# Strassen's seven products for a feed-forward output matmul, with weight combinations streamed from device memory

## The chip, the cores and the metric

One core of one Trainium2 chip runs the kernel. Its engines work side by side: TensorE (PE; its weight loads are listed apart as PEld), VectorE (DVE), ScalarE (ACT), GpSimd (POOL) and SyncE (SP), whose queue issues all DMA transfers here. The metric is the device time of one execution in microseconds (us). A time is a median of several runs. The profile comes from one further execution, and sums are made against that one's own time.

## The reference

Linear attention over 8 batches x 8 heads x 576 tokens x 64 dimensions, then a feed-forward layer with the Mish activation over the 4608 tokens that it gives. All arrays are float32.

```python
def phi(x):
    proj = np.einsum('bhsd,df->bhsf', x, w_phi)               # 128 features
    proj = proj - np.max(np.abs(proj), axis=-1, keepdims=True)
    return np.concatenate([np.exp(proj), np.exp(-proj)], axis=-1)
q_p, k_p = (phi(q), phi(k))
kv = np.einsum('bhsf,bhsd->bhfd', k_p, v)
z = np.sum(k_p, axis=2)
num = np.einsum('bhsf,bhfd->bhsd', q_p, kv)
den = np.einsum('bhsf,bhf->bhs', q_p, z)[..., None] + 1e-06
x = num / den                                                 # as 4608 tokens x 512
h = x @ w_in                                                  # 512 x 2048
sp = np.where(h > 20.0, h, np.log1p(np.exp(np.minimum(h, 20.0))))
out = (h * np.tanh(sp)) @ w_out                               # 2048 x 512
```

## The kernel before

**Tiling.** The 4608 tokens are 18 chunks of 256. For each chunk `c` the layer makes 16 feature tiles of 128 (`in c f`): `h` = `w_in` times `x`, 12 matmuls of 256 columns. Two tiles share a PSUM bank, and for each such pair ACT applies Mish (`mish`, giving `u`). `out c f` multiplies the tile's features with 128 rows of `w_out` into two banks `o`, one for each 128 tokens of the chunk, 512 columns wide, which add up over all 16 tiles. `evict` copies them out and `store` sends them off.

**Three products for one.** Both matmuls of the layer work on numbers split in a high part, rounded to a shorter float, and a low part, the rest: `gh` is a rounding cast of `u` on ACT, `gl` is `u - gh` on DVE, and high x high, high x low and low x high are added. The weights are split once, early in the run, on DVE and ACT, from the 64-bit words in which they come. Each piece of `w_out` lies in SBUF as a tile `wout` of high and low part side by side, 128 x 2 x 512, for all the run.

**Attention** runs beside the layer, in units: 36 units of keys (`k0` to `k35`) and 18 x 2 units of queries (`q c g`). A unit is loaded (`raw`), projected on PE into two banks (`pp`), centred on DVE (maxima `m`, then `e`) and put through two exponentials on ACT. For keys, `sum` adds up products with `v` in a bank `kvps`, one bank for each of the 32 pairs of heads and batches, which DVE copies to `kv`. For queries, `e` is first transposed: DVE transposes blocks, and a round trip through device memory (`there`) sorts them. Then `num` makes two banks of products with `kv`, DVE divides, and another round trip, a cast on ACT and a subtraction on DVE give `xTh` and `xTl`, which `h` reads. In the steady part one unit of queries and one of keys go by for every four pairs of feature tiles.

**Banks.** PSUM has eight: four `att` (attention's), two `h` (the layer's first product, and some projections) and two `o`.

**Order.** Nothing is scheduled while it runs. Each step is a task with an engine, a key (a place on a common scale, one unit for each feature tile), a duration, tasks it depends on, and ring places that it takes and gives back. `Plan.order` plays the tasks through once, and the program is written down in the order found. Each engine follows its own list strictly, and so does SP's queue of transfers: whoever waits holds up all that stands behind it.

## Time and profile before

| | |
|---|---|
| median of 3 runs | 1082.2 us (1082.09 to 1083.13) |
| the profiled execution | 1082.3 us, of which 1080.5 us from its first to its last instruction |
| mean granted TensorE clock | 0.996 |
| PE busy | 1061.9 us, 98% |
| DVE busy | 539.9 us, 50% |
| ACT busy | 666.3 us, 62% |
| data moved by DMA | 120.11 MB, mean 111 GB/s |

A matmul's busy time in the groups of instructions (282 ns for 256 columns) overlaps with the next one's, since they are pipelined. What one costs in a row of them is read from the chain in order of time, where a piece of twelve has its length. In rows, `h<-xTh,win` stands for an output tile and the tiles read, `128x256` for partitions x elements, `x12` for a count, and what stands behind `<-` in brackets for whom the engine waited.

### The profile page before, as it was taken

Reading aid. Unit: us, or ns where it says so; the run is one execution under the profiler, and the core shown is the slowest. Engines: PE = TensorE matmul, PEld = TensorE weight load, DVE = VectorE, ACT = ScalarE, POOL = GpSimd, SP = SyncE. Lnnn points to the kernel's source line nnn. Section 1 sums busy time; section 2 is a strip of 40 time slices with the busy share of each in tenths; the row PEclk is TensorE's granted clock in tenths of the full one; section 3 lists DMA queues with packets and bytes.
Section 4 is the critical chain, followed back from the end, with each engine's and each line's share of the span. In section 5 each row is a group of like instructions: output and inputs, shape, how many; then the busy total and the mean of one; then the engine's idle time right before and its main releaser. Section 6 shows DMA issues by size and latency. Waiting matters only on the chain.

```text
span 1080.5 us, 26883 instructions
## 1 busy us (share of the span) xinstructions
PE 1061.9 (98%) x11272; PEld 963.2 (89%) x11272; DVE 539.9 (50%) x1184; ACT 666.3 (62%) x1013; POOL 0.7 (0%) x6
## 2 busy tenths in 40 slices
PE   7799999999999999999999999999999999999998
PEld 7789988899999999999999999999999999889897
DVE  7899997444444544443444444444444443434211
ACT  6598998656666666666666666666666664444412
POOL 0000000000000000000000000000000000000000
PEclk9899999999999999999999999999999999999999
DMA  9568743333232223232323223232323222222100
GB/s 354 203 233 288 272 137 122 100 92 111 92 110 76 92 87 102 78 102 86 101 91 98 93 91 99 91 111 79 104 78 107 62 83 83 92 77 92 35 20 20
DMA packets 94009, 120.11 MB, mean 111 GB/s; under 512 B 10432, under 2 KB 56640, under 8 KB 93888
## 3 DMA queue, kind: packets, MB, share of 16 engines
q1 hardware_dynamic: 93888, 118.38, 33.1%
q8 instruction: 89, 1.46, 0.6%
q14 instruction: 32, 0.26, 0.1%
HBM read 85.31 MB, written 33.03 MB: 110 GB/s over the span
## 4 chain that ended last, share of the span: by engine, by line
PE 89%; ACT 6%; DVE 3%; issue 1%; DMA 1%; SPq 0%; ACTq 0%; DVEq 0%
PE h L445 34%; PE o L480 34%; PE kvps L289 7%; PE num L289 6%; PE pp_q L266 3%; PE pp_k L266 3%; ACT L451 1%; ACT u L451 1%; ACT wout L234 1%; ACT L182 1%; PE dt L350 0%; ACT gh L454 0%; DMA raw_k<-kT 0%; ACT w_out L182 0%; ACT e_q L360 0%
## 5 line engine op out<-in xcount | busy, mean ns | idle before, releaser
L445 PE MATMUL h<-xTh,win 128*128 128x256 f32 x2304 | 460.3, 282 | 1.3 <-ACT u L451 1.3
L445 PEld LDWEIGHTS h<-xTh,win 128*128 128x128 f32 x2304 | 374.0, 188 | 17.0 <-ACT u L451 1.5
L480 PE MATMUL o<-wout,gh 128*128 128x512 f32 x1152 | 362.3, 395 | 0.6 <-ACT wout L234 0.6
L445 PE MATMUL h<-xTl,win 128*128 128x256 f32 x1152 | 324.9, 282 | 0.3 <-DVE xTl L429 0.3
L462 DVE TENSOR_TENSOR gl<-u,gh 128x256 fp32r<-128x256 f32 x288 | 111.4, 422 | 389.3 <-ACT gh L454 386.9
L480 PE MATMUL o<-wout,gl 128*128 128x512 f32 x576 | 226.8, 394 | 0.0
L445 PEld LDWEIGHTS h<-xTl,win 128*128 128x128 f32 x1152 | 216.4, 188 | 10.7 <-DVE xTl L429 0.5
L480 PEld LDWEIGHTS o<-wout,gh 128*128 128x128 f32 x1152 | 197.3, 188 | 29.3 <-ACT wout L234 1.3
L324 ACT ACT_TABLE_LOAD x50 | 64.2, 1283 | 202.4 <-DVE e_k L281 201.9
L451 ACT ACTIVATE u<-h 128x512 f32<-128x512 f32 x144 | 86.2, 599 | 140.5 <-PE h L445 124.1
L480 PEld LDWEIGHTS o<-wout,gl 128*128 128x128 f32 x576 | 108.0, 187 | 26.6
L451 ACT ACT_TABLE_LOAD x94 | 120.6, 1283 | 1.7
L454 ACT CAST gh<-u 128x256 fp32r<-128x256 f32 x288 | 105.4, 404 | 7.9
L289 PEld LDWEIGHTS kvps<-v,e_k 128*64 128x64 f32 x2560 | 77.9, 137 | 9.6 <-issue 6.5
L289 PE MATMUL kvps<-v,e_k 128*64 128x66 f32 x2560 | 82.8, 223 | 1.6 <-issue 1.6
L289 PE MATMUL num<-kv,e_q 128*64 128x66 f32 x2304 | 76.5, 224 | 0.5 <-ACT e_q L360 0.5
L289 PEld LDWEIGHTS num<-kv,e_q 128*64 128x64 f32 x2304 | 72.2, 139 | 4.3 <-ACT e_q L360 1.5
L324 ACT ACTIVATE e_k<-e_k 128x512 f32<-128x512 f32 x72 | 45.3, 629 | 8.3 <-DVE e_k L281 7.8
L273 DVE TENSOR_REDUCE m_k<-pp_k 128x4 f32<-128x512 f32 x72 | 45.9, 677 | 7.5 <-PE pp_k L266 7.4
L266 PE MATMUL pp_k<-w_phi,raw_k 64*128 64x128 f32 x560 | 44.5, 292 | 4.5 <-DMA raw_k<-kT 4.5
L325 ACT ACTIVATE e_k<-e_k 128x512 f32<-128x512 f32 x72 | 45.5, 632 | 2.3
L266 PEld LDWEIGHTS pp_k<-w_phi,raw_k 64*128 64x128 f32 x560 | 40.8, 201 | 6.0 <-issue 4.8
(59 smaller groups left out, 725.5 us busy)
## 6 DMA issues: line engine op xcount, KB each, us to landing
there_e<-e_q SPq DMA_DIRECT2D x60, 256.0 KB, 2.1
e_q<-there_e SPq DMA_DIRECT2D x240, 64.0 KB, 2.0
v<-va SPq DMA_DIRECT2D x32, 330.0 KB, 3.4
raw_q<-qT SPq DMA_DIRECT2D x36, 256.0 KB, 3.0
out<-osb SPq DMA_DIRECT2D x36, 256.0 KB, 2.1
raw_k<-kT SPq DMA_DIRECT2D x35, 256.0 KB, 3.0
words_in<-w_in SPq DMA_DIRECT2D x16, 512.0 KB, 6.0
words_out<-w_out SPq DMA_DIRECT2D x16, 512.0 KB, 4.9
```

Of the source, the lines that this page charges most:

```text
L182: nc.scalar.activation(w.bitcast(F32), high.bitcast(F32), AF.Abs)
L234: nc.scalar.copy(both((kind, i, j))[0], to_add.pop((kind, i, j)).bitcast(F32))
L266: nc.tensor.matmul(ps[j][:, n], raw[rows, n * P:(n + 1) * P], w_phi2[rows], start=True, stop=True)
L273: nc.vector.tensor_reduce(ms[j], ps[j], axis=AX.X, op=ALU.max, apply_absolute_value=True)
L289: nc.tensor.matmul(ps[rows], lhsT[h], rhs[h], start=start, stop=stop, skip_group_check=True)
L324: nc.scalar.activation(e[:, 1, :], e[:, 0, :], AF.Exp)
L325: nc.scalar.activation(e[:, 0, :], e[:, 0, :], AF.Exp, scale=-1.0)
L445: nc.tensor.matmul(ps, w[:, wcol], x[:, cc % 2, :], start=(n == 0), stop=(n == 11))
L451: nc.scalar.activation(u, h_live.pop((c, fp)).rearrange("p f s -> p (f s)"), AF.Mish)
L454: nc.scalar.copy(gh, u[:, f * CH:(f + 1) * CH])
L462: nc.vector.tensor_sub(gl, u[:, f * CH:(f + 1) * CH], gh.bitcast(F32))
L480: nc.tensor.matmul(ps, g[:, cols], w, start=(i == first and k == 0), stop=(i == end and k == 2))
```

## The change

From chunk 5 on (`FAST`), each pair of feature tiles is seen as a 2 x 2 block product: two blocks of 128 tokens, two of 128 features, two of 256 output columns. Strassen's scheme forms it with seven block products in place of eight. Each is again three matmuls (high and low parts), now 256 columns wide, and adds into one of four banks over the chunk's eight pairs: `x` and `z` take the two `o` banks, `y` and `w` take two of the four `att` banks, which attention gives up from chunk 5 on.

- *Per pair.* ACT: `mish`, one cast `gh` (256 columns: two of the four blocks), one cast `sh` (640 columns: the five sums). DVE: three instructions for the five sums `s`, one `gl`, and `sl` = `s - sh` (640 columns).
- *Per chunk.* ACT copies the `x` bank; DVE combines the four banks with eight additions of 256 columns into `osb0` and `osb1`, which are stored.
- *Weights.* Five combinations of the blocks of `w_out` are needed for each pair. Once, around chunks 1 to 5, DVE and ACT form them and 48 transfers write them to device memory (`terms`). Later each is loaded again for each chunk and pair, 520 loads of 256 KiB, into halves of the `wout` tiles: the scheme uses only one half of each piece, and the other becomes one of 16 homes, filled in turn.
- *Order.* Rings are resized (`part` holds eight places of 640 columns, in place of five of 512; `kv` and `half` lose two places and one). A query or key unit's centring is split in four tasks from step 12 on; a unit's `sum` is one task for each pair of heads, and from pair 11 on the two parts of a pair's sum are made in banks of their own, the second being added to `kv` on DVE. The planner may hold PE up to 0.4 on its scale for the next `sum`, `num` or `project`.

The places on each engine where this shows follow; in the listings `x2` or `x4` merges equal neighbours, and numbers in names are chunk, pair or unit, with a running number last.

TensorE (PE) before, chunk 9, at the end of a group of queries: the last `num` products, the projections of queries `q10_1` and of keys `k26`, and the next feature tile.

```order
L289 MATMUL num1_10_0_7625<-kv_17_5869,e1_q10_0_7325 64x66 x4
L266 MATMUL pp0_q10_1_7647<-w_phi2_81,raw_q10_1_7462 128x128
L266 MATMUL pp1_q10_1_7648<-w_phi2_81,raw_q10_1_7462 128x128
...
L266 MATMUL pp0_k26_7663<-w_phi2_81,raw_k26_7460 128x128
L266 MATMUL pp1_k26_7664<-w_phi2_81,raw_k26_7460 128x128
...
L445 MATMUL h_9_4_7683<-xTh_9_0_7057,win_0_1_1071 128x256
```

TensorE (PE) after, the same place.

```order
L322 MATMUL kvps_23_8470<-v_23_8048,e1_k25_8229 64x66 x4
L493 MATMUL h_9_4_8479<-xTh_9_0_7885,win_0_1_1118 128x256
...
L322 MATMUL num1_10_0_8516<-kv_17_5940,e1_q10_0_8167 64x66 x4
L302 MATMUL pp0_q10_1_8539<-w_phi2_81,raw_q10_1_8324 128x128
L302 MATMUL pp1_q10_1_8540<-w_phi2_81,raw_q10_1_8324 128x128
...
L493 MATMUL h_9_4_8479<-xTh_9_0_7885,win_0_1_1118 128x256
...
L649 MATMUL ow_9_8577<-wout_0_0_851,sl_9_0_8454 128x256
L302 MATMUL pp0_k26_8610<-w_phi2_81,raw_k26_8322 128x128
L302 MATMUL pp1_k26_8611<-w_phi2_81,raw_k26_8322 128x128
```

The keys' projection, which takes both `att` banks, now stands behind a product of the layer, and a feature tile stands between `kvps` and `num`.

SP's queue before, where `x` of the second group of chunk 12 makes its round trip.

```order
L319 DMA v_28_9362<-va 128x660
L297 DMA there_x_12_1_9422<-via_12_1_9402 128x512
```

SP's queue after, the same place.

```order
L352 DMA v_28_10611<-va 128x660
L627 DMA wout_2_0_997<-terms_6_4894 128x2x256
L627 DMA wout_3_0_1052<-terms_7_5189 128x2x256
L330 DMA there_x_12_1_10691<-via_12_1_10674 128x512
L335 DMA x_12_1_10655<-there_x_12_1_10691 32x4x128 x4
L330 DMA there_e0_13_0_10746<-e0_q13_0_10707 128x512
L330 DMA there_e1_13_0_10762<-e1_q13_0_10709 128x512
L627 DMA wout_4_0_1495<-terms_7_5189 128x2x256
```

Streamed loads stand ahead of the round trip and right behind it; each of those waits until TensorE has used what its home held.

The diff, cut to its core:

```diff
-NRAW, NE, NV, NKV, NHALF, NXT, NG, NU, NW, NPART = 2, 4, 2, 10, 3, 6, 4, 2, 3, 5
+NRAW, NE, NV, NKV, NHALF, NXT, NG, NU, NW, NPART = 2, 4, 2, 8, 2, 6, 4, 2, 3, 8
+FAST = 5
+LAGF = 4
+NMIX = 3
+SPLIT_PAIR = 11
+PREP = 40.0
+WIDE = 5 * P
+BURST = ("sum", "num", "project")
+PATIENCE = 0.4
...
+                    if not ready(task):
+                        if held and found is None and task["name"].split()[0] in BURST and soon(task, now + PATIENCE):
+                            break
...
+    def kv_copy(p, more):
+        ps = kv_ps.pop(p)
+        if more:
+            nc.vector.tensor_tensor(kv[p // NHP, p % NHP], ps, kv[p // NHP, p % NHP], op=ALU.add)
+            return
...
+    def mish_fast(c, fp):
+        nc.scalar.activation(u, h_live.pop((c, fp)).rearrange("p f s -> p (f s)"), AF.Mish)
+        nc.scalar.copy(gh.rearrange("p (b m) -> p b m", b=2), blocks(u)[:, 0::3])
...
+    def mix(c, fp):
+        u, s = u_live[c, fp], scratch(f"s_{c}_{fp}", cols=WIDE)
+        b = blocks(u)
+        nc.vector.tensor_tensor(s[:, :CH], u[:, :CH], u[:, CH:], op=ALU.add)
+        nc.vector.tensor_tensor(s[:, CH:2 * CH].rearrange("p (b m) -> p b m", b=2), b[:, 1:3], b[:, 0::3], op=ALU.subtract)
+        nc.vector.tensor_tensor(s[:, 2 * CH:], b[:, 0], b[:, 3], op=ALU.add)
...
+    def mix_cast(c, fp):
+        nc.scalar.copy(mix_high[c, fp], mixed[c, fp])
+    def mix_rest(c, fp):
+        nc.vector.tensor_sub(mix_low[c, fp], mixed.pop((c, fp)), mix_high[c, fp].bitcast(F32))
...
+    def home_of(c, m, i):
+        r = (5 * ((c - FAST) * NFT // 2 + m) + i) % NFT
+        return r, slice(CH, 2 * CH) if r % 2 == 0 else slice(0, CH)
+    def load_term(c, m, i):
+        r, cols = home_of(c, m, i)
+        nc.sync.dma_start(homes_of["out", r, 0].bitcast(F32)[:, :, cols], terms[m][:, i])
+    def out_fast(c, m):
+        if m == 0:
+            names = dict(x="o", z="o", y="att", w="att")
...
+        products = (("x", 0, plain[0], term(3)), ("x", 1, plain[1], term(2)), ("z", 0, summed[4], term(4)),
+                    ("y", 0, summed[0], own(1, slice(CH, 2 * CH))), ("y", 1, summed[1], own(0, slice(0, CH))),
+                    ("w", 0, summed[3], term(1)), ("w", 1, summed[2], term(0)))
+        for k, half, (ah, al), (bh, bl) in products:
+            for n, (a, b) in enumerate(((ah, bh), (ah, bl), (al, bh))):
+                nc.tensor.matmul(ps[k][:, half], a, b, start=(m == n == half == 0), stop=(m == NFT // 2 - 1 and n == 2),
+                                 skip_group_check=True)
...
+    def end_first(c):
+        nc.vector.tensor_tensor(o[0][:, 0], ps["z"][:, 0], s[:, 1], op=ALU.subtract)
+        nc.vector.tensor_tensor(o[1][:, 1], ps["z"][:, 0], s[:, 0], op=ALU.add)
+        nc.vector.tensor_tensor(o[0][:, 1], ps["y"][:, 0], s[:, 0], op=ALU.add)
+        nc.vector.tensor_tensor(o[1][:, 0], ps["y"][:, 1], s[:, 1], op=ALU.subtract)
+    def end_second(c):
+        nc.vector.tensor_tensor(o[0][:, 0], o[0][:, 0], ps["y"][:, 0], op=ALU.subtract)
+        nc.vector.tensor_tensor(o[1][:, 1], o[1][:, 1], ps["y"][:, 1], op=ALU.subtract)
+    def end_third(c, t):
+        nc.vector.tensor_tensor(o[t][:, t], o[t][:, t], ps["w"][:, t], op=ALU.add)
...
+            add(f"term {key} {i}", "SP", n + 0.5 + LAGF - 6.0 + 0.1 * i, 0.42, lambda i=i: load_term(c, m, i),
+                deps=deps + [f"send {m} {min(i // 2, 2)} {p}" for p in range(2)], take=[(f"hs{r}", f"hs:{q}")], size=262144,
+                after=[loaded[q - NFT]] if q >= NFT else [])
...
+        take = [("o", f"ox:{c}"), ("o", f"oz:{c}"), ("fast", f"oy:{c}"), ("fast", f"ow:{c}")] if m == 0 else []
+        if c == FAST and m == 0:
+            take += [("att", "reserved 0"), ("att", "reserved 1")]
+        add(f"out {key}", "PE", when, 2.48, lambda: out_fast(c, m), deps=[f"low {key}", f"mixl {key}"] + [d for d, _ in uses], after=[before_out],
+            take=take, give=[f"g:{key}", f"mix:{key}", f"sh:{key}", f"sl:{key}"] + [t for _, t in uses])
```

## The prediction

> **What bounds the kernel now.** I read the page's head and its chain of waits first, then the busy times by stretch, then the chain in order of time, and last the groups of instructions by shape.

> ```profile
> span 1080.5 us, 26883 instructions
> PE 1061.9 (98%) x11272; PEld 963.2 (89%) x11272; DVE 539.9 (50%) x1184; ACT 666.3 (62%) x1013; POOL 0.7 (0%) x6
> PE 89%; ACT 6%; DVE 3%; issue 1%; DMA 1%; SPq 0%; ACTq 0%; DVEq 0%
> PE h L445 34%; PE o L480 34%; PE kvps L289 7%; PE num L289 6%; PE pp_q L266 3%; PE pp_k L266 3%; ACT L451 1%; ACT u L451 1%; ACT wout L234 1%; ACT L182 1%; PE dt L350 0%; ACT gh L454 0%; DMA raw_k<-kT 0%; ACT w_out L182 0%; ACT e_q L360 0%
> ```

> The chain is TensorE's own work, and a third of the span (`o`) is the product that the change rewrites. The stretches (columns: PE, weight loads, DVE, ACT, POOL, granted clock, DMA share, GB/s) say the same:

> ```profile
> 100.00:150.00 50.00, 49.81 (x434) 44.87 (x434) 46.74 (x111) 47.25 (x71) 0.00 (x0) 1.00 0.68 227
> 150.00:200.00 50.00, 48.25 (x554) 42.84 (x553) 38.75 (x83) 39.26 (x59) 0.00 (x0) 1.00 0.33 108
> 500.00:557.95 57.95, 57.95 (x627) 52.92 (x626) 25.94 (x56) 36.91 (x55) 0.00 (x0) 1.00 0.30 95
> ```

> From 500 to 557.95 us, one steady chunk, TensorE is never idle, DVE works 45%, ACT 64%, DMA 30% of the time. So time removed from TensorE is time removed from the run, until one of the others gets late. From 100 to 150 us DVE and ACT are 93% and 94% busy and DMA 68%, and TensorE still is at 49.81 of 50: busy helpers alone need not stall it.

> ```profile
> 505.03 2.02 PE kvps L289 x64
> 507.05 1.88 PE num L289 x64
> 508.93 1.09 PE pp_q L266 x16
> 510.02 1.06 PE pp_k L266 x15
> 511.08 1.62 PE h L445 x12
> 512.71 1.39 PE o L480 x6
> 514.10 1.42 PE h L445 x12
> 529.55 2.80 PE o L480 x12
> 1076.74 0.69 DVE osb L498
> ```

> These pieces of the chain (start, length, what, matmuls) carry the prices. Twelve matmuls of 256 columns take 1.42 us, 118.3 ns each; twelve of 512 take 2.80 us, 233.3 ns each. Half the columns cost half the time, to 3.3 ns.

> **The change, part by part.**

> *The product.* A pair of feature tiles now costs 12 matmuls of 512 columns, 2.80 us. It will cost 7 products x 3 matmuls = 21 of 256 columns, 21 x 118.3 = 2.48 us. There are 13 chunks x 8 pairs = 104 pairs: 104 x 0.315 = **-32.8 us**. I price the new matmuls by `h`, which has their shape and a weight load for each:

> ```profile
> L445 PE MATMUL h<-xTh,win 128*128 128x256 f32 x2304 | 460.3, 282 | 1.3 <-ACT u L451 1.3
> L445 PEld LDWEIGHTS h<-xTh,win 128*128 128x128 f32 x2304 | 374.0, 188 | 17.0 <-ACT u L451 1.5 <-ACT xTh L423 0.2
> ```

> A load lasts 188 ns and matmuls still start every 118 ns, so loads are hidden, and 21 loads in place of 12 cost nothing. If they showed, there would be no gain, which is a rival below. [...]

> *More changes of product kind on TensorE.* After an `h` or `o`, 64 `kvps` matmuls take 2.02 us; `num` behind `kvps`, with 64 of the same shape, takes 1.88. The first `h` behind `pp` takes 1.62, others 1.42. A trip into these 64-row products and back so costs 0.14 + 0.20 = 0.34 us. In the whole order TensorE makes 56 such trips before and 74 after (the projection of the keys stands apart from that of the queries now, and some sums stand alone): 18 x 0.34 = **+6.1 us**. No row suggests less.

> *The hand-over of two banks.* From chunk 5 on, attention has two `att` banks in place of four. `num` needs the bank that `kvps` has just filled, and the projection one that the first `num` filled. What stands between them is on DVE:

> ```profile
> 506.17 0.43 DVE L341 COPY kv<-kvps 128x264 f32<-128x264 f32 x1 [0.47 <-PE kvps L289]
> 508.04 0.16 DVE L393 TENSOR_SCALAR r<-num 128x4 f32<-128x4 f32 x1 [1.44 <-PE num L289]
> 508.45 0.42 DVE L395 TENSOR_TENSOR x<-num,r 128x256 f32<-128x256 f32 x1
> 517.93 0.69 DVE L429 TENSOR_TENSOR xTl<-x,xTh 128x512 fp32r<-128x512 f32 x1 [1.40 <-ACT xTh L423]
> ```

> The first division ends at 508.87 and the projection starts at 508.93: the hand-over would just fit if DVE were waiting for it. From below it costs 0; from above, a DVE instruction of up to 0.69 us is in the way at each of three hand-overs, 2.1 us x 26 groups of queries = 54 us. I take 0.15 us a group, **+3.9 us**, near the lower end, since DVE's rows show it idle and waiting before two of these instructions (0.47 and 1.44 us).

> *DVE.* Lengths by shape:

> ```profile
> L462 DVE TENSOR_TENSOR gl<-u,gh 128x256 fp32r<-128x256 f32 x288 | 111.4, 422 | 389.3 <-ACT gh L454 386.9
> L429 DVE TENSOR_TENSOR xTl<-x,xTh 128x512 fp32r<-128x512 f32 x30 | 20.8, 692 | 50.2 <-ACT xTh L423 50.2
> L498 DVE COPY osb<-o 128x512 f32<-128x512 f32 x31 | 20.2, 683 | 7.4 <-PE o L480 7.4
> L395 DVE TENSOR_TENSOR x<-num,r 128x256 f32<-128x256 f32 x72 | 30.6, 424 | 2.5
> ```

> 256 columns take 422 ns and 512 take 692, so by the same slope 128 take 287 and 640 take 827 (estimates). A pair had two `gl`, 0.84 us. Now it has three sums (422 + 422 + 287), one `gl` and the low part (827): 2.38 us, +1.54. A chunk gains 8 x 1.54 = 12.3, eight end additions of 0.424 instead of two copies of 0.683 (+2.0), and two additions to `kv` (about +0.9): 25.9 becomes 41.1 of 55.4 us, 74%. The weight combinations (8 x some 5.1 us = 41 us) stand spread from chunk 1's later tiles to chunk 5 in DVE's order. That is some 145 us of work for TensorE at 45% use, so there is room. Their cover is this idle DVE, and I cost them at nothing. If DVE falls behind there, TensorE waits for `gl`.

> *ACT.*

> ```profile
> L454 ACT CAST gh<-u 128x256 fp32r<-128x256 f32 x288 | 105.4, 404 | 7.9
> L423 ACT CAST xTh<-x 128x512 fp32r<-128x512 f32 x30 | 18.3, 611 | 15.4 <-DMA x<-there_x 15.2
> L451 ACT ACT_TABLE_LOAD x94 | 120.6, 1283 | 1.7
> ```

> Two casts of 0.404 become one, plus one of 640 columns (715 ns by the slope): +0.31 a pair, 2.5 a chunk, and 0.6 for the copy of the `x` bank. The order holds 146 table loads instead of 188, 54 us less over the run, 3 to 4 a chunk. ACT stays near 37 of 55 us. Cost 0, covered by its own idle third. What is new is that ACT's cast of the sums waits for DVE, with the next `mish` queued behind it.

> *DMA and its queue.* 520 loads of 256 KiB, 10.5 MB a chunk. The stretches moved 95 GB/s at a share of 0.30 and 227 at 0.68, so a full share moves 317 to 334 GB/s: 31 to 33 us a chunk beside the 17.4 (0.30 x 57.95) there now, 88% to 91% of 55.4 us. [...] Sixteen half homes give a load three pairs of lead, about 18 us, against some 3 us of landing:

> ```profile
> raw_q<-qT SPq DMA_DIRECT2D x36, 256.0 KB, 3.0
> there_x<-via SPq DMA_DIRECT2D x30, 256.0 KB, 2.0
> x<-there_x SPq DMA_DIRECT2D x120, 64.0 KB, 1.9
> ```

> I cost the loads at 0, hidden by that lead. Behind them on SP stand the round trips of `x` and `e_q`, which have no such lead (a rival). Issue takes about 0.4 us each, 16 us more a chunk, and leaves SP room. The 48 sends of the combinations have some 100 us before their first use: 0.

> *The end.* Today one copy of 0.69 us follows the last matmul. Now the `y` products end 6 x 0.118 = 0.71 us before the last one, and six additions of 0.424 must follow: 2.54 - 0.71 = 1.83 us. **+1.1 us**; up to +1.9 if the first sums are late.

> *The ramp.* Other pool sizes and split sums reorder the first 200 us, where TensorE's busy time falls short of the span by most of 1080.5 - 1061.9 us. Without a row that shows a sign I take 0, within 5 us either way.

> Sum, from the profiled execution's 1082.3 us (the median of the runs is 1082.2): 1082.3 - 32.8 + 6.1 + 3.9 + 1.1 = **1060.6 us**.

> **The rivals.**

> 1. *The bank hand-overs stall.* DVE at 74% is often in the middle of something: three hand-overs x 0.74 x half of 0.69 us = 0.77 us a group, x 26 = 20 us instead of 3.9, **1077 us**. For it: two banks, and a DVE that waits for ACT in order. Against it: DVE's work there is placed right behind the products, and 100 to 150 us shows a DVE at 93% with TensorE at 49.81 of 50.

> 2. *The streamed loads make `x` late; slower than before.* In the rows above the second group's products end at 508.93 and its `xTl` at 518.62, 9.7 us later, with two DMA hops between. In the new order two `h` pairs' worth of time, two new products and two projections follow (1.1 + 2.84 + 2.48 + 1.3 + 2.84 + 2.48), then half of the first `h` tile, 0.7: 13.7 us until TensorE needs it. The slack is 4 us. Five streamed loads are 1.31 MB, 4.1 us at 317 GB/s. If such a batch lies ahead of one hop, it just fits; ahead of both it is 8.2 us, and TensorE waits 4.2 us in each of 13 chunks, 55 us: **1115 us**. It decides for slower once the wait exceeds 21.7 / 13 = 1.7 us a chunk. Against it: in SP's order the send and the fetch of the second group's `x` stand next to each other, behind two or three loads, and no product frees a home while attention's products run.

> 3. *A fixed cost for each matmul or weight load shows*, so that 21 matmuls cost as much as 12: no gain, and the 11.1 us of the other terms stay, **1093 us**. [...]

> 4. *Nothing is late and the trips overlap or the ramp gains:* 1082.3 - 32.8 + 1.1 = 1051 us, less up to 5 from the ramp.

> **How the numbers follow.** My forecast (1054 to 1069) has 0.60, rival 1 (1069 to 1080) 0.18, rival 4 (under 1054) 0.09, rival 2 0.09 with most of it above 1085, rival 3 0.01; 0.03 is left for a mixture that ends level. Faster by over 0.2% (2.2 us, about what a measurement here can tell) is 0.87, level 0.03, slower 0.10. The range 1049 to 1078 holds the forecast, most of rivals 1 and 4, and leaves out the rest of these with rivals 2 and 3. The predicted time is the forecast's 1060.6.

> **What would show it.** In the chain by time, 21 matmuls of the new product should take 2.45 to 2.50 us (about 3 says rival 3). TensorE's idle time after chunk 5 should be under 10 us, with `num` and `pp_q` waiting for DVE in pieces of about 0.2 us; pieces of 0.7 or more are rival 1. An `h` that waits 2 to 4 us for `xTl` once a chunk, or an `o` product that waits for a `wout` load, is rival 2. DVE should be near 780 us in all (540 + 104 x 1.54 + 13 x 2.9 + 41), ACT near 665, the DMA share near 0.8 to 0.9 in a steady chunk. The prediction is wrong if TensorE's idle time grows by over 27 us.

## The result and the profile after

The changed kernel takes 1132.2 us (median of four runs, 1130.7 to 1134.6) against 1082.1 us before on the same chip. The ratio is 1.046, with a 95% interval of 1.044 to 1.048: slower by 4.6%, where 1060.6 us was forecast.

The head of the profile after (line numbers are those of the changed kernel: L649 is the new product, L493 is `h`, L322 makes `kvps` and `num`, L302 projects):

```profile
span 1128.9 us, 29827 instructions
...
PE 1063.0 (94%) x12208; PEld 1006.1 (89%) x12208; DVE 729.8 (65%) x1668; ACT 662.3 (59%) x1007; POOL 0.7 (0%) x6
...
PE 38%; DVE 18%; DMA 17%; ACT 16%; SPq 6%; issue 4%; ACTq 0%; DVEq 0%
```

TensorE's share of the chain that ended last fell from 89% to 38%. The rest went to DVE, DMA and ACT, which had had 3%, 1% and 6%. No engine is busier than TensorE; more than before, the handing on from one to the next sets the time. A steady chunk, in the columns shown before:

```profile
685.00:747.00 62.00, 58.25 (x737) 56.38 (x735) 38.59 (x91) 34.84 (x51) 0.00 (x0) 1.00 0.82 254
```

A chunk takes 62 us in place of 58. DVE works 62% of it, ACT 56%, DMA 82%, and TensorE, which had not paused, lacks 3.75 us. The new product itself is what the sum said. The chain in order of time has one whole pair of feature tiles:

```profile
474.76 0.73 PE ox L649 x6
475.49 0.37 PE oz L649 x3
475.86 0.68 PE oy L649 x6
476.54 0.68 PE ow L649 x6
```

The 21 matmuls take 0.73 + 0.37 + 0.68 + 0.68 = 2.46 us; 2.48 was forecast. So the loss is not in the product, but in what DVE, ACT and TensorE wait for:

```profile
DVE sl L578 <- ACT sh L574: 76.3, 47, 6.0
ACT xTh L471 <- DMA x<-there_x: 69.6, 26, 5.3
...
PE num L322 <- DVE kv L386: 24.8, 16, 2.4
ACT L403 <- DMA e_q<-there_e: 24.1, 17, 3.8
```

The columns are the total wait, how often, and the longest. TensorE waits most for the second half of `kv` (L386, the addition that the change brought). ACT waits 69.6 us for `x` to land, where before it was 15.2, and 24.1 us for `e_q`. DVE's 76.3 us for ACT's cast `sh` are the largest of these rows, but not the largest loss: without the streamed loads (the first experiment) DVE still waits 59.4 us there, and TensorE hardly pauses. These are the landings, in the last column:

```profile
wout<-terms SPq DMA_DIRECT2D x520, 256.0 KB, 5.6
there_e<-e_q SPq DMA_DIRECT2D x60, 256.0 KB, 3.3
e_q<-there_e SPq DMA_DIRECT2D x240, 64.0 KB, 2.5
raw_q<-qT SPq DMA_DIRECT2D x36, 256.0 KB, 5.0
there_x<-via SPq DMA_DIRECT2D x30, 256.0 KB, 3.1
x<-there_x SPq DMA_DIRECT2D x120, 64.0 KB, 3.4
```

Both hops of `x`, 2.0 and 1.9 us before, take 3.1 and 3.4, and `raw_q` takes 5.0 in place of 3.0. A landing is counted from its issue, and a part of the delay lies ahead of that. In this program each of SP's transfers tells of its end by the semaphore (the counter that others wait for) that the transfer eight places ahead of it used, and is issued only when that one has landed: of 1212 transfers of the trace none was issued before that (the smallest distance is 0.02 us), while 364 were issued with the one seven places ahead still under way. This held the fetches of the round trips (L335) back 50 times:

```profile
SPq L335 <- DMA wout<-terms: 38.5, 50, 2.3
```

The kernel before has no such row. One such place lies on the chain that ended last: a fetch of `e_q` was issued at 581.73 us, when the load eight places ahead of it, issued at 575.53, had landed. One pass of the chain in order of time shows how such a landing comes to stop TensorE:

```profile
479.78 0.40 SPq L627
...
481.82 0.47 SPq L627
482.40 0.40 SPq L335
...
483.79 4.60 DMA e_q<-there_e
488.45 1.28 ACT L403
...
490.95 0.71 ACT sh L574
...
494.17 0.61 ACT u L559
...
498.10 0.73 DVE sl L578
498.84 0.35 DVE kv L386
499.24 1.16 PE num L322 x32
500.39 2.48 PE h L493 x12
```

SP issues five streamed loads (L627) and then the fetch of `e_q` (L335). The fetch takes 4.60 us behind them. ACT, which had just waited for `x`, waits again at its exponential L403, and `sh` and `mish` stand behind that in ACT's list:

```profile
480.36 0.62 ACT L471 CAST xTh<-x 128x512 fp32r<-128x512 f32 x1 [3.20 <-DMA x<-there_x]
488.45 1.28 ACT L403 ACT_TABLE_LOAD   x1 [1.33 <-DMA e_q<-there_e]
```

DVE waits 3.68 us for `sh` and 2.28 us for the next `u`. Then it makes the sums and low parts of two pairs in one go, 4.0 us from 494.80 on; the addition to `kv` stands behind them in its list, and TensorE's `num` needs `kv`. So late data and DVE's new work add up on this path. The last piece shows what comes on top: twelve `h` in 2.48 us, which took 1.42 before (the section on the hardware tells why).

**Where the 48 us went.** I added up, over all matmuls in the trace, the time from one start to the next, with pauses counted apart. From before to after the output products went from 404.3 to 380.1 us (-24.2), `h` from 416.4 to 423.3 (+6.9), attention's products from 231.2 to 249.6 (+18.4), pauses from 10.6 to 56.8 (+46.2). That makes +47.3 of the span's +48.4. The sums of the products include what stretches at half clock added to them.

### The profile page after: what moved, and what is told of

Same layout as the page of the kernel before. It is cut to its first block, busy times and chain, and to the rows that moved or that the text cites. A ratio compares the mean times of both kernels' runs of the same rounds, so it can differ in the third digit from the quotient of the medians.

```text
span 1128.9 us, 29827 instructions
## 1 busy us (share of the span) xinstructions
PE 1063.0 (94%) x12208; PEld 1006.1 (89%) x12208; DVE 729.8 (65%) x1668; ACT 662.3 (59%) x1007; POOL 0.7 (0%) x6
## 3 DMA queue, kind: packets, MB, share of 16 engines
q1 hardware_dynamic: 246336, 265.22, 73.7%
## 4 chain that ended last, share of the span: by engine, by line
PE 38%; DVE 18%; DMA 17%; ACT 16%; SPq 6%; issue 4%; ACTq 0%; DVEq 0%
PE h L493 14%; PE o L528 6%; DMA e_q<-there_e 5%; PE num L322 4%; DMA wout<-terms 4%; PE kvps L322 3%; DMA x<-there_x 3%; SPq L335 3%; ACT L559 3%; DVE sl L578 2%; PE pp_q L302 2%; ACT L403 2%; ACT e_q L403 2%; SPq L627 2%; PE pp_k L302 2%
## 5 line engine op out<-in xcount | busy, mean ns | idle before, releaser
L493 PE MATMUL h<-xTh,win 128*128 128x256 f32 x2304 | 448.1, 285 | 1.3 <-ACT u L559 0.9
L493 PEld LDWEIGHTS h<-xTh,win 128*128 128x128 f32 x2304 | 368.9, 190 | 11.6 <-ACT u L559 1.6
L493 PE MATMUL h<-xTl,win 128*128 128x256 f32 x1152 | 325.4, 282 | 0.7 <-DVE xTl L477 0.7
L493 PEld LDWEIGHTS h<-xTl,win 128*128 128x128 f32 x1152 | 219.2, 190 | 3.2 <-DVE xTl L477 1.1
L578 DVE TENSOR_TENSOR sl<-s,sh 128x640 fp32r<-128x640 f32 x104 | 85.4, 822 | 77.4 <-ACT sh L574 76.3
L322 PE MATMUL num<-kv,e_q 128*64 128x66 f32 x2304 | 82.8, 230 | 27.5 <-DVE kv L386 24.8
L322 PEld LDWEIGHTS num<-kv,e_q 128*64 128x64 f32 x2304 | 76.0, 143 | 33.8 <-DVE kv L386 27.2
L574 ACT CAST sh<-s 128x640 fp32r<-128x640 f32 x104 | 74.6, 723 | 52.9 <-DVE s L569 52.4
L528 PE MATMUL o<-wout,gh 128*128 128x512 f32 x320 | 101.9, 399 | 1.5 <-ACT gh L502 0.7
L322 PEld LDWEIGHTS kvps<-v,e_k 128*64 128x64 f32 x2560 | 78.6, 138 | 8.7 <-issue 5.1
L322 PE MATMUL kvps<-v,e_k 128*64 128x66 f32 x2560 | 83.7, 224 | 2.1 <-issue 2.1
L649 PE MATMUL ox<-wout,gh 128*128 128x256 f32 x416 | 79.3, 282 | 1.0 <-DMA wout<-terms 1.0
L649 PE MATMUL oy<-wout,sh 128*128 128x256 f32 x416 | 77.5, 280 | 0.0
L649 PE MATMUL ow<-wout,sh 128*128 128x256 f32 x416 | 77.3, 279 | 0.0
L528 PEld LDWEIGHTS o<-wout,gh 128*128 128x128 f32 x320 | 55.6, 188 | 12.2 <-ACT gh L502 1.1
L649 PEld LDWEIGHTS ox<-wout,gh 128*128 128x128 f32 x416 | 63.9, 188 | 1.2 <-issue 1.2
L649 PEld LDWEIGHTS oy<-wout,sh 128*128 128x128 f32 x416 | 63.7, 189 | 0.0
L649 PEld LDWEIGHTS ow<-wout,sh 128*128 128x128 f32 x416 | 63.5, 189 | 0.0
L528 PE MATMUL o<-wout,gl 128*128 128x512 f32 x160 | 63.2, 395 | 0.0
## 6 DMA issues: line engine op xcount, KB each, us to landing
wout<-terms SPq DMA_DIRECT2D x520, 256.0 KB, 5.6
there_e<-e_q SPq DMA_DIRECT2D x60, 256.0 KB, 3.3
raw_q<-qT SPq DMA_DIRECT2D x36, 256.0 KB, 5.0
out<-osb SPq DMA_DIRECT2D x36, 256.0 KB, 3.7
raw_k<-kT SPq DMA_DIRECT2D x35, 256.0 KB, 4.3
```

Of the source, the lines that this page charges most:

```text
L322: nc.tensor.matmul(ps[rows], lhsT[h], rhs[h], start=start, stop=stop, skip_group_check=True)
L493: nc.tensor.matmul(ps, w[:, wcol], x[:, cc % 2, :], start=(n == 0), stop=(n == 11))
L528: nc.tensor.matmul(ps, g[:, cols], w, start=(i == first and k == 0), stop=(i == end and k == 2))
L574: nc.scalar.copy(mix_high[c, fp], mixed[c, fp])
L578: nc.vector.tensor_sub(mix_low[c, fp], mixed.pop((c, fp)), mix_high[c, fp].bitcast(F32))
L649: nc.tensor.matmul(ps[k][:, half], a, b, start=(m == n == half == 0), stop=(m == NFT // 2 - 1 and n == 2), skip_group_check=True)
```

## The experiments

The theories. A: the streamed loads' bytes stand in front of the small round trips of `x` and `e_q` in SP's queue, and what comes late there passes through ACT's and DVE's order to TensorE. A has a wide form (the mean DMA share slows everything) and a narrow one (what counts is the loads right ahead of a hop). B: DVE's added work, or the two banks. C: the loads' places and issue time in SP's list, not their bytes. Where no interval stands, a kernel had one run, beside one of the kernel before at 1082.5 or 1082.6 us. "Pauses" are TensorE's gaps after the first 60 us, added up from the trace: 2.5 us in the kernel before, 49.4 in the changed one.

**Without the loads.** The homes keep what they hold; all else stays.

```diff
-        nc.sync.dma_start(homes_of["out", r, 0].bitcast(F32)[:, :, cols], terms[m][:, i])
+        return
```

> The 520 streamed loads are left out; the products read what lies in the homes. Order, banks, DVE's and ACT's work stay. Theory A (the bytes of the streamed loads slow the round trips of x and e_q, ACT waits for these in its order, the casts sh, then sl and kv on DVE come late, and num on TensorE waits): about 1065 us, TensorE's idle time under 12 us and no more clock drops. Theory B (DVE's added work and the two banks are the cause, loads are hidden): 1120 to 1132 us. Theory C (not bytes, but the loads' places in SP's queue, where they wait for homes and cost issue time): about 1065 us too; the next run tells A from C.

Measured: 1068.8 us, pauses of 8.5 us. A steady chunk:

```profile
651.00:708.00 57.00, 57.00 (x724) 55.64 (x721) 38.51 (x89) 34.86 (x51) 0.00 (x0) 1.00 0.29 91
```

DVE and ACT work as much as after (38.5 and 34.9 us), and TensorE never pauses. The loads cost 63 us in all. With DVE just as busy and the banks the same, B alone can't be the cause of more than what is left. It can still make a late piece of data dearer, as in the pass above.

**A quarter of the bytes.** All 520 loads stay at their places, each for 32 partitions of 128.

```diff
-        nc.sync.dma_start(homes_of["out", r, 0].bitcast(F32)[:, :, cols], terms[m][:, i])
+        nc.sync.dma_start(homes_of["out", r, 0].bitcast(F32)[:32, :, cols], terms[m][:32, i])
```

> Each streamed load moves 32 of 128 partitions: a quarter of the bytes and packets, with every load still issued at its place, with its waits. The other partitions keep old data. Theory A (bytes): 1065 to 1080 us, landing of x back near 1.9 us. Theory B (DVE and banks): 1120 to 1132. Theory C (places and issue time in SP's queue): 1110 to 1132, since nothing there has changed.

Measured: 1073.5 us, pauses of 11.9 us, and landings nearly as before the change:

```profile
wout<-terms SPq DMA_DIRECT2D x520, 64.0 KB, 2.2
...
x<-there_x SPq DMA_DIRECT2D x120, 64.0 KB, 2.0
```

Places and issue time cost at most some 5 us, the 4.7 that separate this from the run without loads. C falls as the main cause; the other 59 us come with the bytes (and with the packets that carry them, which fall from 272 to 80 a load). Loads this short no longer hold a fetch back either: the row of L335 waiting for `wout` is gone.

**Fewer loads.** Every second chunk takes its pairs in reverse, so that three pairs' combinations are still at home and 340 loads do (core of the edit).

```diff
+    def pairs(c):
+        m = list(range(NFT // 2))
+        return m[::-1] if c >= FAST and (c - FAST) % 2 else m
...
-        r = (5 * ((c - FAST) * NFT // 2 + m) + i) % NFT
+        r = 5 * slot_of[c, m][0] + i
...
+            if slot_of[c, m][1]:
```

> The same computation, but every second chunk takes its pairs of feature tiles from the last to the first, so that three of eight pairs find their combinations still in the homes: 340 loads in place of 520. Theory A: the DMA share of a steady chunk falls from 0.83 to about 0.63 and over half of the loss comes back, 1070 to 1095 us. Theory C: loads fall by a third and so does the loss, about 1105. Theory B: 1125 to 1135.

Measured: 1134.5 us, no gain. The first row is the queue's total after, the others are of this run:

```profile
q1 hardware_dynamic: 246336, 265.22, 73.7%
```

```profile
q1 hardware_dynamic: 197376, 218.02, 60.7%
...
ACT xTh L471 <- DMA x<-there_x: 73.7, 24, 5.3
```

A share of 60.7% in place of 73.7% left ACT's wait for `x` where it was, against what theories A and C expected; the time lies in theory B's range, which the run without loads has ruled out as the cause. That speaks against the wide form of A, but not by itself: the order was written anew for this run, and another order alone is worth 32 us in a run below. The next two runs keep the order.

**Near loads or far loads.** In SP's order, 194 loads stand within four loads ahead of a hop of `x` or `e_q`; the other 326 stand farther off. One run quarters the bytes of the near, the other those of the far.

```diff
+            if kind == "term":
+                near[tuple(int(x) for x in rest)] = since < AHEAD
+                since += 1
+            elif kind in ("send", "turn", "out") and rest[0][0] == "q":
+                since = 0
...
+        n = 32 if near[c, m, i] == True else P
+        nc.sync.dma_start(homes_of["out", r, 0].bitcast(F32)[:n, :, cols], terms[m][:n, i])
```

> Same order as the changed kernel. 194 of the 520 streamed loads, those that stand within four loads ahead of a hop of a round trip (send or fetch of x or e_q) in SP's queue, move a quarter of their bytes; the other 326 stay whole. The share of DMA falls only from 0.83 to about 0.70. Theory A in its narrower form (what counts is the bytes that lie right ahead of a round trip in the same queue): about 1075 to 1090 us, most of the loss gone. Its wide form (mean DMA share counts): about 1115. Theory B: 1125 to 1132.

> The complement: the other 326 loads move a quarter, the 194 right ahead of a hop stay whole. The DMA share falls to about 0.60. Narrow form of theory A: 1110 to 1130 us, though more bytes are taken away. Wide form: 1090 or less. Theory B: 1125 to 1132.

Measured: near loads small 1078.3 us, pauses of 16.2; far loads small 1102.7 us, pauses of 31.0. The second hop of `x`, first of the run with the near ones small:

```profile
x<-there_x SPq DMA_DIRECT2D x120, 64.0 KB, 2.0
```

and of the run with the far ones small:

```profile
x<-there_x SPq DMA_DIRECT2D x120, 64.0 KB, 3.2
```

Quartering the near loads removes 194 x 0.196 = 38 MB and brings back 53.9 us. Quartering the far ones removes 326 x 0.196 = 64 MB, more bytes, and brings back 29.5 us. So place counts as well as bytes: the narrow form of A holds in the main, and the wide one falls. The second run missed both ranges, though (1110 to 1130, and 1090 or less): far loads cost more than the narrow form has it. The fetches that were held back for a load follow the place too: 1.4 us in all with the near ones small, 30.0 with the far ones small. The two savings add up to 83 us, more than the 63 there are to have, so the two groups' costs overlap.

**DVE's largest new instruction left out.** `sl` isn't made, and `sh` stands in for it.

```diff
-        mix_low[c, fp] = scratch(f"sl_{c}_{fp}", F32R, WIDE)
-        nc.vector.tensor_sub(mix_low[c, fp], mixed.pop((c, fp)), mix_high[c, fp].bitcast(F32))
+        mix_low[c, fp] = mix_high[c, fp]
+        mixed.pop((c, fp))
```

> The subtraction that makes sl (640 columns, 0.82 us on DVE, 104 times) is left out, the high part sh stands in for it; loads as in the changed kernel. Theory B (DVE's work is the cause): about 85 us less on DVE and half the loss gone, 1095 to 1105 us. Theory A: round trips stay as late; only the 0.8 us of sl ahead of the kv addition goes from each of 16 waits, 1110 to 1122.

Measured: 1118.1 us, pauses of 44.8 us. With 79 us of DVE's work gone (650.4 us busy in place of 729.8), and with it the wait for `sh` ahead of the addition to `kv`, only 14 us come back, as theory A had it. ACT's wait for `x` stays:

```profile
ACT xTh L471 <- DMA x<-there_x: 82.1, 27, 5.7
```

**The loads on another queue.** GpSimd issues them.

```diff
-        nc.sync.dma_start(homes_of["out", r, 0].bitcast(F32)[:, :, cols], terms[m][:, i])
+        nc.gpsimd.dma_start(homes_of["out", r, 0].bitcast(F32)[:, :, cols], terms[m][:, i])
```

> All bytes are loaded, but the 520 loads are issued from GpSimd's queue, which does nothing else; SP keeps the round trips, and the planner writes the order anew with this. If loads hold round trips up because they stand ahead of them in one queue (narrow A), this helps most: 1065 to 1095 us. If it is the DMA engines' sharing of bytes, whatever the queue: 1110 to 1135. A loss is possible if GpSimd's way of issuing is slow: 520 issues at over 2 us each would make the loads themselves late and TensorE would wait for wout.

Measured: 1185.2 us, the slowest of all and outside both ranges.

```profile
wout<-terms POOLq DMA_DIRECT2D x520, 256.0 KB, 4.3
...
e_q<-there_e SPq DMA_DIRECT2D x240, 64.0 KB, 4.3
...
x<-there_x SPq DMA_DIRECT2D x120, 64.0 KB, 4.5
```

The loads no longer stand ahead of a hop in SP's queue, no fetch is held back for one, and the hops land still later, 4.5 us in place of 3.4. So standing in one queue is not what it took here; loads under way at the same time were enough. "Near" in the runs above was near in the queue and near in time at once, and those runs can't tell the two apart. The loads come late as well: TensorE waits 25.4 us for them at the first product of a pair, where it had waited 1.0. The mean granted clock falls from 0.985 to 0.966, by an estimate from the span of 1183.3 us some 22 us of the time. The run is no clean exchange of queues: its order is another, and its loads go in 80 packets each in place of 272.

**A plan that knows of slower transfers.** The order was found with 400 GB/s and at least 2.4 us from issue to landing.

```diff
-                    bus = max(bus, now + 1.0) + found["size"] / 400e3
-                    late = max(bus - now - took, 2.4)
+                    bus = max(bus, now + 1.0) + found["size"] / (300e3 if now > 400 else 400e3)
+                    late = max(bus - now - took, 3.4 if now > 400 else 2.4)
```

> Same instructions; only the planner's price of a transfer is raised from the place 400 on (300 GB/s in place of 400, at least 3.4 us to land in place of 2.4), so that the written order leaves round trips more time. Theories A and C: the engines no longer stand in line for late transfers and 15 to 40 us come back, 1092 to 1117 us. Theory B: no gain, 1125 to 1140.

Measured: 1100.6 us, pauses of 34.4 us, with the same 520 loads and a queue share of 75.6%. The two hops of `x` take 3.9 and 3.1 us, together no less than the changed kernel's 3.1 and 3.4, and yet ACT's wait for `x` goes from 69.6 to 41.0 us. TensorE's wait for the second half of `kv` falls from 24.8 to 3.2. So 32 of the 50 us lost come back by another order alone. That it is the later places of ACT's and DVE's steps is the likeliest reason, but SP's list changed with them.

**Loads held back from the round trips.** While a round trip is under way in the plan, no load is put into SP's list.

```diff
+            if task["name"][:5] == "term " and held_back():
+                return False
```

> The changed kernel with one rule added to the order: while a round trip of x or of e_q is under way in the plan (up to 8 us of it), no streamed load is put into SP's queue. All 520 loads and all their bytes stay. Theory (bytes that stand right ahead of a round trip make it late): x lands in about 2.2 to 2.6 us in place of 3.4, the wait of the cast xTh for x falls from 69.6 us to under 30, TensorE's visible idle time from 49 to under 30, and the time is 1075 to 1100 us; not as low as the 1078 of the run with the near loads quartered, since the loads, pressed into the gaps, can come late themselves. Rival (the mean DMA share of 0.86 is what counts): no gain, 1125 to 1135.

Measured: 1137.8 us, ratio 1.050 (1.048 to 1.052). The expectation of 1075 to 1100 is missed by far. ACT's wait for `x` falls only to 47.0 us (under 30 expected), and pauses rise to 57.6. Fetches are hardly held at their issue any more (2.9 us for loads), so that alone did not make the loss. The second hops land as they had before the change, and the first hop of `x` doesn't:

```profile
e_q<-there_e SPq DMA_DIRECT2D x240, 64.0 KB, 2.0
...
there_x<-via SPq DMA_DIRECT2D x30, 256.0 KB, 3.2
x<-there_x SPq DMA_DIRECT2D x120, 64.0 KB, 2.0
```

The queue's timeline (start, length, what) and the chain show why:

```profile
641.48 4.48 SPq L639 DMA_DIRECT2D wout<-terms  x9
...
648.23 8.86 SPq L639 DMA_DIRECT2D wout<-terms  x11
657.53 0.33 SPq L342 DMA_DIRECT2D there_x<-via  x1
```

```profile
657.53 5.87 DMA there_x<-via
```

Twenty loads are now pressed into the gap ahead of the send, which takes 5.87 us behind them. And what was moved becomes late itself: TensorE's wait for `wout` at a pair's first product goes from 1.0 to 17.8 us. That 520 loads leave the queue no empty place to move them to is how I read this; the next run, with fewer, fits it.

**Held back, and fewer.** The last rule with the reversed pairs: two edits, neither of which brought anything by itself.

> The rule of the run before and the pairs in reverse in every second chunk, so that 340 loads do in place of 520. The second half brought nothing by itself (1134.5 us). Theory: with the round trips clear of loads there is now room in the gaps for the 340 that are left, so x lands in about 2.1 to 2.4 us, TensorE idles 12 to 25 us, and the time is 1068 to 1088 us, level with the kernel before or faster. Rival (fewer bytes never help, nor does their place): 1125 or more.

Measured: 1108.6 us, ratio 1.024 (1.022 to 1.025), pauses of 35.8 us: 20 us outside the expected range but 24 us below the changed kernel. The two hops of `x` now land in 2.2 and 2.0 us. Fewer loads leave gaps, and the rule uses them.

**With the slower transfers in the plan too** (300 GB/s and 2.8 us from 400 us on).

> As the run before, and the plan also reckons with slower transfers from 400 us on (300 GB/s and at least 2.8 us in place of 400 GB/s and 2.4 us), so that ACT and DVE have their steps on x and e_q later in their lists. Theory: what waits are left on landings (ACT's on x and e_q) go from some 20 us to under 10, TensorE idles 8 to 18 us, 1064 to 1080 us: faster than before, and near the 1073.5 of the run with a quarter of the bytes. Rival: the later steps hold TensorE as long as the waits did, 1080 to 1100.

Measured: 1090.4 us, ratio 1.006 (1.005 to 1.008), pauses of 23.3 us: above the theory's 1064 to 1080, in the rival's range. ACT's waits did go as the theory had it, from 30.2 us for `x` in the run before to 2.3, and from 11.9 us for `e_q` to 7.1. TensorE's pauses did not follow them below 18. What TensorE waits for now is `raw` and `wout`, not steps put later, so the rival's reason isn't seen either. All of the way from 1132 to 1090 is order and the number of loads; the full result is still computed.

**Loads of `raw` and `v` first.**

```diff
+            if task["name"][:5] == "term " and (held_back() or any(
+                    t["name"][:4] == "load" and t["key"] < task["key"] + 2.0 and soon(t, now + 2.5) for t in waiting["SP"][:48])):
```

> The run before (held-back loads, pairs in reverse, slower transfers in the plan; 1090.4 us) with one more rule: a streamed load is also held back in the plan while a load of raw or v can go within 2.5 us. In the run before, the first chunk of the new product took 75.1 us against 63.9 in the run without loads, with TensorE waiting 3.0 us for raw_k and 2.4 us for wout there. Theory (what is left is still small transfers behind batches of loads): the wait of pp_k for raw_k, 4.5 us in all, goes to under 2, raw lands in 3 to 4.5 us in place of 4.9 to 5.5, and the time is 1080 to 1088 us. Rival (the queue is full while the first homes are filled, so whatever goes first makes something else late): the waits move to wout, 1088 to 1096.

Measured: 1091.8 us (1087.3 to 1097.4), ratio 1.010 (1.007 to 1.013): no difference from the run before that these runs could tell. The theory missed: the projection of the keys still waits 5.6 us for `raw_k` (under 2 expected), and `raw` lands in 4.8 to 5.0 us. The time lies in the rival's range, but the waits did not move to `wout` as the rival had it; TensorE's wait for that fell from 6.9 to 3.2 us:

```profile
PE pp_k L315 <- DMA raw_k<-kT: 5.6, 2, 4.0
...
PE h L506 <- ACT xTh L484: 4.0, 3, 2.1
PE ox L678 <- DMA wout<-terms: 3.2, 6, 1.0
```

They are spread, with 4.6 us for `raw_q`, over four releasers. No version that computes the full result beat the kernel before. The gap of the last version but one (1090.4) to the run without loads is 21.6 us; 11 of them lie in the first chunk of the new product, which runs 75.1 us from chunk 4's first write into `osb` to its own, against 63.9 without loads. Of these, 6 us are pauses, 3.0 for `raw_k` and 2.4 for `wout` the longest. The rest of the 11 stays open.

## Why the prediction was wrong

**The step that failed** is "I cost the loads at 0, hidden by that lead." The lead held for the loads: TensorE waited 1.0 us for `wout` in the whole run. It didn't hold for what stands behind them in the queue: from the end of DVE's transposition to the landing of `x`, a round trip took 5.5 us before and 9.6 after (medians from 400 us on). Worth: 63 us (1132.2 against 1068.8 without the loads), where the sum had nothing.

**Rival 2 was the right mechanism with a wrong path and chance.** It said that five loads ahead of both hops make `x` late, 1115 us, and got 0.09. Both hops did become slow. But it looked for the wait where `x` is used, at `h`, and gave it 4 us of slack. `h` waited for `xTl` and `xTh` about 1 us in all. The wait ended one engine earlier: ACT's cast stands in ACT's list, and `sh` and the next `mish` behind it have less slack than `h`. `e_q`, named beside `x` and not priced, ran the same way. The prediction's sign for this rival, an `h` or an `o` that waits, therefore didn't show; what showed was its sign for rival 1, `num` waiting for DVE in pieces of over 0.7 us (24.8 us in 16 pieces of up to 2.4). The run without loads settles it: 0.5 us of that wait is left. The argument against it, that the send and the fetch stand next to each other "behind two or three loads", was the mistake in short: two or three loads of 262 KB at the 254 GB/s of this chunk are 2 to 3 us for each hop (the medians rose by 1.1 and 1.5), and the near loads alone brought back 54 us. That a fetch can also be held at its issue, 38.5 us in all, stands nowhere in the prediction. How much of the 63 us is this and how much is slower landing, no run separates.

**What the sum missed altogether** is the clock, in the section on the hardware: by estimate some 12 us, in stretches that came behind pauses. Most of it is a part of the 63: without the loads the mean granted clock was 0.993 in place of 0.985, an estimated 9 us of the span of 1128.9.

**The other terms** can be read from the run without loads, by the same count from start to start:

| term | predicted | measured without loads |
|---|---|---|
| product | -32.8 us | -29.8 us (119.1 ns a matmul on the mean, 2.50 us for 21; the `o` of chunks 0 to 4 also slowed from 234.1 to 238.4 ns) |
| trips into the 64-row products | +6.1 us | +8.9 us (attention's products 231.2 to 240.1 us) |
| bank hand-overs | +3.9 us | within +5.7 us of pauses; 3.2 us were one wait for `raw_q` |
| tail behind the last matmul | +1.1 us | +0.9 us (0.73 us before, 1.67 after) |

Together they gave 1068.8 us where 1060.6 was forecast: the change without its transfers is worth 14 us against the 1082.6 beside it. Weight loads (medians of 188 to 192 ns in the new product) and a fixed cost for each matmul don't show in the 119.1 ns, so rival 3 is wrong. Rival 1's stalls at the banks aren't there either: without loads, DVE's work at the hand-overs stands behind some 3 us of the pauses, and 20 were its price.

**Which signs were right.** DVE 729.8 us (780 forecast: each instruction took what the slope gave, 417, 285 and 822 ns, but neighbours overlap, and three sums in a row take 0.43 + 0.34 + 0.20 = 0.97 us in the chain in place of 1.12), ACT 662.3 (665), DMA share 0.82 (0.8 to 0.9), and the condition for being wrong, idle time that grows by over 27 us (it grew by 47). A forecast DMA share of 0.88 to 0.91 stood in the text, and no cost was drawn from it.

## What to carry to other kernels

A transfer that lands in time can still be dear (here 63 us for loads that TensorE waited 1.0 us for): price it by what stands behind it or runs beside it, and above all by two-hop round trips, which pay twice (here 1.1 and 1.5 us). Look also at when a transfer is issued, not only at how long it takes from there (fetches were held 38.5 us). Where engines keep a fixed order, as here, the slack of a late piece of data is that of the next instruction behind its first reader, not that of its last user. An order found by playing through a plan is as good as the plan's transfer times: when a change doubles the traffic, change these as well.

## What the runs showed of the hardware

```profile
496.50:499.20 2.70, 0.34 (x12) 0.20 (x8) 2.70 (x7) 1.44 (x3) 0.00 (x0) 1.00 1.10 359
500.80:504.20 3.40, 3.40 (x37) 3.18 (x37) 2.04 (x8) 0.00 (x0) 0.00 (x0) 0.50 0.92 330
504.20:508.00 3.80, 3.80 (x48) 3.61 (x45) 3.04 (x7) 0.63 (x2) 0.00 (x0) 1.00 0.23 87
```

In the 3.41 us ahead of each of the seven stretches TensorE had paused 1.5 to 2.3 us in sum; one pause of 2.37 us, at 427.9, had no such stretch behind it. The seven begin whole multiples of 3.41 us apart, and cut into windows of that grid the pause at 427.9 falls on two, with 1.2 us of idle time in one and 1.5 in the other. In this trace, after the first 100 us, every window with 1.8 us or more had a half clock behind it; of those with less, only one had, with 1.46 us. So the windows ahead of the seven stretches were idle for 0.43 to 0.66 of their length. From 500.39 to 502.87 us the mean granted clock was 0.58, and the twelve `h` there took 2.48 us in place of 1.42. From this and the length, each stretch costs by estimate up to 3.41 / 2 = 1.7 us, some 12 us in all. What sets a half clock off, beyond these idle times, no run shows.

**Another queue was no other lane.** With the same loads issued from GpSimd, in fewer packets (80 a load in place of 272) and in another order, the second hop of `x` on SP's queue was slower: 4.5 us in place of 3.4.
